# Two places of a fused FNet and MLP kernel rewritten: the first rows' way in, and the last column stage's order and stores

## The chip, the cores and the metric

The kernel runs on one core of a Trainium2 chip. The metric is the time of one execution on the device, in microseconds. TensorE (PE) multiplies, VectorE (DVE) and ScalarE (ACT) work on its results in PSUM and on SBUF, and SyncE (SP), ACT and GpSimd (POOL) issue the DMA transfers. Each engine runs its own list of instructions in order and waits on semaphores for the others.

## The reference

```python
def _A_ref(x, dft_seq_re, dft_seq_im, dft_hid_re, dft_hid_im):
    a = jnp.einsum("bsd,ed->bse", x, dft_hid_re)
    b = jnp.einsum("bsd,ed->bse", x, dft_hid_im)
    return jnp.einsum("ts,bse->bte", dft_seq_re, a) - jnp.einsum("ts,bse->bte", dft_seq_im, b)

def _B_ref(x, w1, b1, w2, b2):
    h = _gelu(jnp.einsum("bsd,df->bsf", x, w1) + b1)
    return jnp.einsum("bsf,fd->bsd", h, w2) + b2

xn = _layernorm(x, axis=-1)
return x + _A_ref(xn, ...) + _B_ref(xn, B_w1, B_b1, B_w2, B_b2)
```

x is 1 x 2048 x 640, the MLP's inner width 1536, and all is float32.

## The kernel before

**Head.** x comes in chunks of 128 rows, four to a tile. `load_x` (called in L698 and L699) loads chunks c0 to c3, the even ones on SP's queue, the odd ones on ACT's; behind them on SP go pieces of the first weight (`load_w1`, L258). PE runs twelve `warm_up` products of zeros (L715). The four chunks are centered (c0, c2 and c3 by `center` on DVE, L744; c1 on ACT), and 20 PE transposes of 128 x 128 (`transpose_x`, L732) put the centered rows into five PSUM banks `tacc[j]`, one for each 128 columns, with all four chunks side by side. `split` (L162 on ACT, L163 on DVE) then makes of each bank two fp32r numbers, a rounded half and the rest, and the first products (L302) read those. `split_first` (L765 on ACT, L766 on DVE) splits the first weight in the same way. Centers of c2 and c3 are made in two parts, columns 0 to 255 of both, and then, behind the weight's first split, the rest.

**Products.** A float32 product is made of three fp32r matmuls (L281, L282, L283: half by half, and the two cross terms), each with 512 columns of the moving operand and a 128 x 128 stationary one. The Fourier transform of the normed rows is made in stages: "s" stages transform along the sequence, "y" stages along the hidden width. Each stage is a 2 x 2 block product done with seven products (`NW` = 7) in place of eight, so that sums and differences of the blocks have to be formed beside it. `entries` lists (stage, product w, piece u); the loop at the end of the kernel goes through it: PE's matmuls (`sequence_entry` or `hidden_entry`), then the split of the piece three entries later (`form`, into one of the three buffers `as`), then the additions, transposes, loads and stores that `beside` or `hidden_beside` put at this entry. What stands in the code first is first in each engine's list.

A "y" stage has 21 entries: seven products of three pieces with 2, 2 and 1 of the five 128-row positions. The products sum into PSUM banks: X, Y and Z of two banks each, and US and VS of one. w = 0 and 1 also sum into US, w = 2 and 6 into VS. Matrices for a product at a position come through `load_g` in the order of the list `G`. In the last stage, w = 6 is done bank by bank: VS, then X, then X + 1, each with 15 matmuls of 512 columns.

**Tail.** `store` (L1372) writes a piece of a result block with four transfers, one for each quarter of the partitions, on the queues that it is given. Results of two row blocks (`ya` and `yo`, and the columns `ys` of the second) are added to what comes transposed out of PSUM by DVE (`turned`, `add_turned`). After the last matmul, the loop in L1825 to L1832 turns bank X + 1 whole and stores it. The framework gives each transfer of SP and ACT one of eight completion counters (DMAHW0 to DMAHW7), in the order of the code, and lets it wait for the transfer before it on that counter.

## Time and profile before

| | before |
|---|---|
| runs, median of 3 | 849.54 us (849.43 to 849.59) |
| the profiled execution | 849.81 us |
| its span | 848.0 us |
| instructions | 10383 |
| mean granted TensorE clock | 0.999 |

The page describes one execution. The span runs from its first instruction to its last, and 1.81 us of the profiled execution lie outside it. Busy time is given for each engine; PEld is PE's loading of the stationary operand, which overlaps the matmuls. The chain of work follows the last instruction back to what released it.

### The profile page before, as it was taken

The page shows a single profiled execution, that of the slowest core. Times are in us where ns is not written, and L with a number is a line of the kernel's source. Part 1 is how long each engine was busy: PE and PEld are TensorE (multiplying, and loading weights), DVE is VectorE, ACT ScalarE, POOL GpSimd, SP SyncE. Part 2 cuts the span into 40 slices and gives each one's busy share as a digit, 9 for nine tenths or more (in the row PEclk, how much of TensorE's full clock was granted, in tenths as well). Part 3 has the DMA queues.
Part 4 walks back from the last instruction along what each step waited for, and adds up shares of the span by engine and source line. Part 5 has one row for each costly group of instructions (what it writes and reads, how often), then busy time and mean ns, then how long its engine had stood idle before and what let it go on. Part 6 is the DMA issues. An engine that isn't in the chain of part 4 may idle for free.

```text
span 848.0 us, 10383 instructions
## 1 busy us (share of the span) xinstructions
PE 841.8 (99%) x3722; PEld 696.9 (82%) x3722; DVE 667.2 (79%) x855; ACT 355.7 (42%) x499; POOL 49.8 (6%) x70
## 2 busy tenths in 40 slices
PE   9999999999999999999999999999999999999997
PEld 8888888888888888888888888888888888888886
DVE  6765875686758878779988887889967988885687
ACT  7453644455665645433444343232323433223241
POOL 0000311031221400000000000000000000000001
PEclk9999999999999999999999999999999999999999
DMA  6758799537679989858644579563865779805364
GB/s 187 213 161 210 161 252 257 137 87 199 196 249 364 348 180 181 167 142 184 147 140 110 161 240 289 141 149 101 207 163 171 252 187 229 310 19 180 124 169 110
DMA packets 202435, 158.45 MB, mean 187 GB/s; under 512 B 75984, under 2 KB 175824, under 8 KB 201872
## 3 DMA queue, kind: packets, MB, share of 16 engines
q1 hardware_dynamic: 193696, 135.25, 62.1%
q0 software_dynamic: 4144, 21.24, 6.4%
q10 hardware_dynamic: 4544, 1.31, 0.6%
q8 instruction: 29, 0.48, 0.2%
q14 instruction: 22, 0.18, 0.1%
HBM read 114.76 MB, written 42.99 MB: 186 GB/s over the span
## 4 chain that ended last, share of the span: by engine, by line
PE 98%; DVE 1%; DMA 0%; issue 0%; DVEq 0%
PE banks L281 29%; PE banks L282 29%; PE banks L283 29%; PE banks L320 9%; PE banks L302 1%; DMA x<-in_A_x_dram 0%; DVE st L187 0%; DVE xp L744 0%; PE banks L352 0%; PE banks L355 0%; PE banks L353 0%; PE banks L732 0%; DVE yo L1829 0%; DVE mv L188 0%; PE banks L812 0%
## 5 line engine op out<-in xcount | busy, mean ns | idle before, releaser
L281 PE MATMUL banks<-as,xab 128*128 128x512 f32 x411 | 159.9, 389 | 0.0
L283 PE MATMUL banks<-as,xab 128*128 128x512 f32 x411 | 159.9, 389 | 0.0
L282 PE MATMUL banks<-as,xab 128*128 128x512 f32 x411 | 159.9, 389 | 0.0
L162 ACT ACTIVATE as<-r 128x1024 fp32r<-128x1024 f32 x80 | 85.0, 1062 | 177.7 <-PE banks L283 149.5
L163 DVE TENSOR_TENSOR as<-r,as 128x1024 fp32r<-128x1024 f32 x80 | 97.2, 1216 | 42.0 <-ACT as L162 42.0
L283 PEld LDWEIGHTS banks<-as,xab 128*128 128x128 f32 x411 | 77.2, 188 | 16.1
L281 PEld LDWEIGHTS banks<-as,xab 128*128 128x128 f32 x411 | 77.2, 188 | 16.0
L282 PEld LDWEIGHTS banks<-as,xab 128*128 128x128 f32 x411 | 77.2, 188 | 16.0
L281 PE MATMUL banks<-as,xc 128*128 128x512 f32 x224 | 87.1, 389 | 0.0
L282 PE MATMUL banks<-as,xc 128*128 128x512 f32 x224 | 87.1, 389 | 0.0
L283 PE MATMUL banks<-as,xc 128*128 128x512 f32 x224 | 87.1, 389 | 0.0
L162 ACT ACTIVATE as<-rt 128x1024 fp32r<-128x1024 f32 x32 | 34.0, 1063 | 70.5 <-PE banks L283 62.5
L320 PE MATMUL banks<-xtt,xab 128*128 128x512 f32 x210 | 50.0, 390 | 0.0
L283 PEld LDWEIGHTS banks<-as,xc 128*128 128x128 f32 x224 | 42.1, 188 | 8.8
L282 PEld LDWEIGHTS banks<-as,xc 128*128 128x128 f32 x224 | 42.1, 188 | 8.7
L281 PEld LDWEIGHTS banks<-as,xc 128*128 128x128 f32 x224 | 42.0, 188 | 8.7
L320 PEld LDWEIGHTS banks<-xtt,xab 128*128 128x128 f32 x210 | 39.4, 188 | 8.1
L163 DVE TENSOR_TENSOR as<-rt,as 128x1024 fp32r<-128x1024 f32 x32 | 38.8, 1212 | 5.3 <-ACT as L162 5.3
L162 ACT ACTIVATE as<-u 128x1024 fp32r<-128x1024 f32 (+1 forms) x24 | 22.1, 919 | 48.2 <-PE banks L283 48.2
L553 DVE STREAM_TRANSPOSE r<-raw 128x1024 f32<-128x1024 f32 x32 | 39.5, 1239 | 2.8 <-PE banks L283 2.2
L163 DVE TENSOR_TENSOR as<-u,as 128x1024 fp32r<-128x1024 f32 (+1 forms) x24 | 24.9, 1042 | 18.8 <-ACT as L162 18.8
L553 DVE STREAM_TRANSPOSE rt<-raw 128x1024 f32<-128x1024 f32 x32 | 38.8, 1230 | 0.9 <-PE banks L283 0.8
(364 smaller groups left out, 1635.7 us busy)
## 6 DMA issues: line engine op xcount, KB each, us to landing
raw<-in_A_dft_seq_re_dram SPq DMA_DIRECT2D x64, 256.0 KB, 5.4
raw<-in_A_dft_seq_im_dram SPq DMA_DIRECT2D x64, 256.0 KB, 5.0
ws<-wit SPq DMA_DIRECT2D x15, 384.0 KB, 5.0
xs<-x SPq DMA_DIRECT2D x64, 80.0 KB, 1.9
xo<-in_A_x_dram SPq DMA_DIRECT2D x16, 320.0 KB, 6.5
xab<-wit SPq DMA_DIRECT2D x13, 384.0 KB, 4.3
wit<-wstp POOLq DMA_DIRECT2D x12, 384.0 KB, 3.3
x<-in_A_x_dram SPq DMA_DIRECT2D x14, 320.0 KB, 4.6
```

The costliest lines, as they stand in the source:

```text
L162: nc.scalar.activation(h, s, AF.Copy)
L163: nc.vector.tensor_tensor(l, s, h.bitcast(F32), op=ALU.subtract)
L281: nc.tensor.matmul(acc, wh, mh, start=first, stop=False, skip_group_check=goes_on)
L282: nc.tensor.matmul(acc, wh, ml, start=False, stop=False, skip_group_check=goes_on)
L283: nc.tensor.matmul(acc, wl, mh, start=False, stop=last, skip_group_check=goes_on)
L302: nc.tensor.matmul(bank(g), W1[g][:, a, j * P : (j + 1) * P], XT[j][:, b], start=(j, k) == ends[0], stop=(j, k) == ends[-1],)
L320: nc.tensor.matmul(acc, W1[i][:, a, j * P : (j + 1) * P], XT[j][:, b], start=n == 0, stop=n == len(steps) - 1)
L553: nc.vector.transpose(held(pieces[g][2], u).rearrange("p c (n i) -> p c n i", i=B), r.rearrange("p n (c i) -> p c n i", i=B))
```

## The change

On the way in, all four chunks of x are loaded by SP; c2 is centered in one instruction, c3 in two, and the first weight's split comes after them; the transposes are taken chunk by chunk, with a warm-up behind c0 and c1. In the last column stage the products are taken in the order 1, 3, 4, 5, 6, 2, 7 (`order_of`). Two differences are formed in the stage before it (`moved_t2`) and kept beside the sums. What was added to a result after its transposition is now transposed early (`turn_ahead`, `turn_odd`) and put into the PSUM bank ahead of the products, by a copy on ACT or an add on DVE, so that the product goes on summing on it (`kept`, `goes_on`). The last product on X + 1 is split into two halves of 256 columns, and so are its transposition and its stores. Stores of `out_a`, of the odd columns and of the last pieces go to SP and ACT in turn; the second columns (`out_b` with k = 1) to SP alone.

```diff
+    def order_of(st):
+        return (0, 2, 3, 4, 5, 1, 6) if st == stages[-1] else tuple(range(NW))
+
+    entries = [(*st, w, u) for st in stages for w in order_of(st) for u in range(2 if st[0] == "s" else 3)]
...
+            src = A.get(("moved", w, u), src)
...
-        load_x(c, nc.scalar if c % 2 else nc.sync)
+        load_x(c)
...
-    def centers(j0, j1):
-        center(2, ALU.subtract, MV[:, 2, 0:1], j0, j1)
-        center(3, ALU.add, MV[:, 3, 5:6], j0, j1)
-
-    centers(0, 2)
+    center(2, ALU.subtract, MV[:, 2, 0:1])
+    center(3, ALU.add, MV[:, 3, 5:6], 0, 2)
+    center(3, ALU.add, MV[:, 3, 5:6], 2, ND)
     split_first(0, 2 * P)
-    centers(2, ND)
-    transpose_x(0, 0, ND)
-    transpose_x(1, 0, ND)
-    warm_up()
-    for j in range(2):
-        transpose_x(2, j, j + 1)
-        transpose_x(3, j, j + 1)
-    for c in (2, 3):
-        transpose_x(c, 2, ND)
+    for c in range(NC):
+        transpose_x(c, 0, ND)
+        if c < 2:
+            warm_up()
...
+            if p == 3:
+                post += {
+                    11: [lambda: turn_ahead(blocks[b - 1][1], 2, A["rt2"][:, 0, 0])],
+                    12: [lambda: turn_ahead(blocks[b - 1][1], 0, A["r01"][:, 0, 0]), lambda: turn_odd(t)],
+                    13: [lambda: moved_t2(b, 1)],
+                }.get(n, [])
...
+    def turn_ahead(t, c, dst):
+
+        nc.vector.transpose(
+            dst.rearrange("p c (n i) -> p c n i", i=B),
+            yo[t][:, :, c * B : (c + 2) * B].rearrange("p n (c i) -> p c n i", i=B),
+        )
+
+    def turn_odd(t):
+        nc.vector.transpose(A["r01"][:, 0, 1, 0].rearrange("p (n i) -> p n i", i=B), yo[t, 4])
+
+    def moved_t2(b, k):
+        t = blocks[b][1]
+        A["moved", 3, k] = A["r01"][:, 1, k]
+        add(A["r01"][:, 1, k], sums[t, KV[k]], sums[t, KU[k]], ALU.subtract)
...
+        def difference(k):
+            return A["moved", 3, k] if last and k < 2 else s(1, KU[k])
+
         def t3(k):
-            return lambda: add(s(0, KU[k]), s(1, KU[k]), s(0, KU[k]), ALU.subtract)
+            return lambda: add(s(0, KU[k]), difference(k), s(0, KU[k]), ALU.subtract)
 
         def t4(k):
-            return lambda: add(s(0, KV[k]), s(0, KV[k]), s(1, KU[k]), ALU.subtract)
+            def f():
+                dst = s(0, KV[k])
+                if last:
+                    dst = A["rt2"][:, (k + 1) // 2, (k + 1) % 2]
+                    dst = A["moved", 6, k] = dst if k < 2 else dst[:, 0]
+                add(dst, s(0, KV[k]), difference(k), ALU.subtract)
+
+            return f
...
+            if last:
+                return A["columns"][:, k]
...
+            return lambda: store(ta, ya[:, :, c0:c1], c0, c1, [nc.sync, nc.scalar] * 2) if last else None
...
+            if last:
+                yt = A["r01"][:, 0, 1, 1]
+                nc.vector.transpose(yt, us)
+                add_turned(ya[:, :, 4 * B :], yt)
+                out_a(4 * B, DQ)()
+                return
             yt = turned(us, f"yo_{tb}")
             add_turned(ya[:, :, 4 * B :], yt)
             add_turned(yo[tb, 4], yt)
-            out_a(4 * B, DQ)()
+
+        def last_odd():
+            nc.vector.transpose(yo[tb, 4], vs.rearrange("p (n i) -> p n i", i=B))
+            add_turned(yo[tb, 4], A["r01"][:, 0, 1, 1])
+            store(tb, yo[tb, 4], 4 * B, DQ, [nc.sync, nc.scalar] * 2)
+
+        def first_pair():
+            nc.vector.transpose(
+                ya[:, :, : 2 * B].rearrange("p n (e i) -> p e n i", i=B), y_.rearrange("p e (n i) -> p e n i", i=B)
+            )
+            out_a(0, 2 * B)()
+
+        def open_columns():
+            A["columns"] = place("xc01", (P, 2, NB, 2 * B), F32, name="columns")
+            load_yb(0)()
+            load_yb(1)()
...
-            return lambda: store(tb, columns(k), 2 * k * B, 2 * (k + 1) * B, [nc.gpsimd] * Q if last else None)
-
-        def last_two():
-
-            acc, yt = s(1, "v1"), A["yt"](f"yb2_{tb}")
-            d = columns(1).rearrange("p n (e i) -> p e n i", i=B)
-            v1()
-            for n in range(2):
-                m = slice(n * TB // 2, (n + 1) * TB // 2)
-                for e in range(2):
-                    nc.vector.transpose(yt[:, e, m], acc[:, e, m])
-                dn = d[:, :, n * NB // 2 : (n + 1) * NB // 2]
-                add(dn, dn, yt[:, :, m].rearrange("p e (n i) -> p e n i", i=B))
-                queues = [nc.sync, nc.scalar] * 2
-                store(tb, columns(1), 2 * B, 4 * B, queues, n * NB // 2, (n + 1) * NB // 2)
-                if n == 0:
-                    end()
-
-        def last_columns():
-
-            A["end"] = A["rt2"][:, 0, 0, 0]
-            nc.vector.transpose(A["end"].rearrange("p (n i) -> p n i", i=B), ya[:, :, 3 * B : 4 * B])
+            return lambda: store(tb, columns(k), 2 * k * B, 2 * (k + 1) * B, [nc.gpsimd] * Q if last and k == 0 else None)
...
-        pre = [v1] if n == 17 and not last else []
+        if last:
+            held0, held4 = A["r01"][:, 0, 0], A["r01"][:, 0, 1, 0]
+            post = {
+                0: [
+                    lambda: gather(1, tb, "v1", z_),
+                    lambda: gather(1, tb, "v", vs, op=ALU.subtract),
+                    lambda: moved_t2(b, 0),
+                ],
+                1: [open_columns, copy(vs, held4), t3(1)],
+                2: [t2(2), t3(0)],
+                3: [lambda: add(held0, held0, x_)],
+                4: [copy(y_, held0), t3(2), t4(1)],
+                5: [t4(0)],
+                6: [copy(s(1, "v1"), z_), t4(2)],
+                9: [copy(s(1, "v2"), x_)],
+                12: [lambda: add(s(1, "v2"), s(1, "v2"), z_)],
+                13: [yb1],
+                14: [yb1],
+                15: [v1, yb2],
+                16: [lambda: add(x_, x_, A["rt2"][:, 0, 0]), yb2],
+                18: [first_pair, odd],
+                19: [last_odd],
+            }.get(n, [])
...
+        g0 = order_of(("y", (blocks[b - 1][1], blocks[b][1]))).index(w) * ND
+
+        def use_g(acc, j, pos, first, stop, goes_on=False, m=slice(0, TB)):
             r, k = (n - u + (pos // 2)) % 3, pos % 2
             a = A["as"][:, r]
-            use(acc, GT[b, w * ND + pos], j, a, k, first, stop, goes_on)
+            use(acc[:, m], GT[b, g0 + pos], j, a[:, :, :, m], k, first, stop, goes_on)
 
         def wide(j, pos):
-            use_g(bank(where + j), j, pos, w < 3 and pos == 0, pos == ND - 1, w > 2)
+            kept = w > 2 or (last and w == 1)
+            use_g(bank(where + j), j, pos, not kept and pos == 0, pos == ND - 1, kept)
...
-                    use_g(bank(VS), 2, pos, False, pos == ND - 1)
+                    use_g(bank(VS), 2, pos, False, pos == ND - 1, True)
                 for pos in range(ND):
                     wide(0, pos)
             elif u == 1:
-                for pos in range(ND):
-                    wide(1, pos)
+                for m in (slice(0, TB // 2), slice(TB // 2, TB)):
+                    for pos in range(ND):
+                        use_g(bank(X + 1), 1, pos, False, pos == ND - 1, True, m)
             return
...
-                use_g(bank(VS), 2, pos, pos == 0, False)
+                use_g(bank(VS), 2, pos, pos == 0 and not last, False, last)
...
     t = blocks[-2][1]
-    for k, queues in ((2, [nc.sync, nc.scalar] * 2), (3, [nc.sync, nc.scalar] * 2)):
+    for k, n0, n1 in ((2, 0, NB), (3, 0, NB // 2), (3, NB // 2, NB)):
         d = yo[t][:, :, k * B : (k + 1) * B]
-        if k == 3:
-            nc.vector.transpose(d, bank(X + 1).rearrange("p (n i) -> p n i", i=B))
-        else:
-            add_turned(d, turned(bank(X), f"yt_{k}"))
-        store(t, d, k * B, (k + 1) * B, queues=queues)
+        nc.vector.transpose(d[:, n0:n1], bank(X + k - 2)[:, n0 * B : n1 * B].rearrange("p (n i) -> p n i", i=B))
+        store(t, d, k * B, (k + 1) * B, [nc.sync, nc.scalar] * 2, n0, n1)
```

How it moves instructions, at three places. In the lists a row is line, operation, result and operand, shape, and how many stand in a row.

PE at the start of the program, up to the first products, as a difference (before -, after +); `zeros` are the warm-ups, `xp` the centered rows, `xtt` the split transposed ones:

```order
-L1859 UNCONDITIONAL_BRANCH
-L715 MATMUL banks<-zeros 128x128 x12
-L732 MATMUL banks<-ident,xp 128x128 x10
-L715 MATMUL banks<-zeros 128x128
-L732 MATMUL banks<-ident,xp 128x128 x10
+L1912 UNCONDITIONAL_BRANCH
+L720 MATMUL banks<-zeros 128x128 x12
+L737 MATMUL banks<-ident,xp 128x128 x5
+L720 MATMUL banks<-zeros 128x128
+L737 MATMUL banks<-ident,xp 128x128 x5
+L720 MATMUL banks<-zeros 128x128
+L737 MATMUL banks<-ident,xp 128x128 x10
```

A warm-up more stands between the transposes, and the blocks of c2 are all ahead of those of c3.

DVE's last instructions, before; `as` is the split's buffer, `v_1_2_5580` the sum whose columns are stored second, in brackets what an instruction waits for:

```order
L163 TENSOR_TENSOR as<-v_1_1_5297,as 128x1024 [waits Activation_49]
L493 TENSOR_TENSOR u_1_2_5314<-u_1_2_5314,yb_2_5961 128x2x16x32 [waits DMAHW0_49,DVE_49]
L163 TENSOR_TENSOR as<-v_1_1_5122,as 128x1024 [waits Activation_49]
L163 TENSOR_TENSOR as<-v_1_5280,as 128x512 [waits Activation_49]
L493 TENSOR_TENSOR v_1_2_5580<-v_1_2_5580,banks 128x1024 [waits PE_49]
```

And after, with the end of the list (L1884 is the loop behind the last product):

```order
L163 TENSOR_TENSOR as<-rt_2826,as 128x1024 [waits Activation_49]
L493 TENSOR_TENSOR banks<-banks,rt_2826 128x1024
L493 TENSOR_TENSOR columns<-columns,yb_2_5962 128x2x16x32 [waits DMAHW5_49,DVE_49]
L163 TENSOR_TENSOR as<-rt_2826,as 128x512 [waits Activation_49]
L1696 STREAM_TRANSPOSE yo_5255<-banks 128x2x16x32
L1682 STREAM_TRANSPOSE r_2747<-banks 128x512 [waits PE_49]
L493 TENSOR_TENSOR yo_5255<-yo_5255,r_2747 128x16x32 [waits DVE_49]
L1691 STREAM_TRANSPOSE y_2_5547<-banks 128x512 [waits PE_49]
L493 TENSOR_TENSOR y_2_5547<-y_2_5547,r_2747 128x512 [waits DVE_49]
L1884 STREAM_TRANSPOSE yo_5255<-banks 128x16x32 [waits PE_49]
L1884 STREAM_TRANSPOSE yo_5255<-banks 128x8x32 [waits PE_49]
L1884 STREAM_TRANSPOSE yo_5255<-banks 128x8x32
```

Two adds of 1024 elements a partition came between the splits of the second and third piece of the last product; of the two transposes of the last bank only the first waits for PE.

SP's last stores, before:

```order
L1372 DMA out_dram<-y_2_5547 32x16x32 [waits DMAHW3_49,DVE_49]
L1372 DMA out_dram<-y_2_5547 32x16x32 [waits DMAHW5_49]
L1372 DMA out_dram<-yo_5255 32x16x32 [waits DMAHW7_49,DVE_49]
L1372 DMA out_dram<-yo_5255 32x16x32 [waits DMAHW1_49]
L1372 DMA out_dram<-yo_5255 32x16x32 [waits DMAHW3_49,DVE_49]
L1372 DMA out_dram<-yo_5255 32x16x32 [waits DMAHW5_49]
```

SP's last six, after:

```order
L1370 DMA out_dram<-yo_5255 32x16x32 [waits DMAHW0_49,DVE_49]
L1370 DMA out_dram<-yo_5255 32x16x32 [waits DMAHW1_49]
L1370 DMA out_dram<-yo_5255 32x8x32 [waits DMAHW2_49,DVE_49]
L1370 DMA out_dram<-yo_5255 32x8x32 [waits DMAHW3_49]
L1370 DMA out_dram<-yo_5255 32x8x32 [waits DMAHW4_49,DVE_49]
L1370 DMA out_dram<-yo_5255 32x8x32 [waits DMAHW5_49]
```

And ACT's last six, after:

```order
L1370 DMA out_dram<-yo_5255 32x16x32 [waits DMAHW6_49,DMAHW5_49,DVE_49]
L1370 DMA out_dram<-yo_5255 32x16x32 [waits DMAHW7_49]
L1370 DMA out_dram<-yo_5255 32x8x32 [waits DMAHW0_49,DVE_49]
L1370 DMA out_dram<-yo_5255 32x8x32 [waits DMAHW1_49]
L1370 DMA out_dram<-yo_5255 32x8x32 [waits DMAHW3_49,DVE_49]
L1370 DMA out_dram<-yo_5255 32x8x32 [waits DMAHW4_49]
```

Before, SP's stores have the odd counters and ACT's the even ones. After, SP has three more of the last stores, two smaller ones stand where one stood, and both queues use the counters 0, 1, 3 and 4.

More of the change, by code (lines that the diff above doesn't have):

```diff
@@ L1567, in beside @@
         return pre, post
+    def turn_ahead(t, c, dst):
[9 more added lines that the diff above has]
+        add(A["r01"][:, 1, k], sums[t, KV[k]], sums[t, KU[k]], ALU.subtract)
     CHUNKS = ((0, 2), (1, 3), (4,))
-    G = [(w, c) for w in range(NW) for cs in CHUNKS for c in cs]
+    G = {
+        b: [(w, c) for w in order_of(("y", (blocks[b - 1][1], blocks[b][1]))) for cs in CHUNKS for c in cs]
+        for b in (NT + 1, NT + 3)
+    }
     GT = {}
@@ L1642, in out_a @@
         def out_a(c0, c1):
-            return lambda: store(ta, ya[:, :, c0:c1], c0, c1) if last else None
+            return lambda: store(ta, ya[:, :, c0:c1], c0, c1, [nc.sync, nc.scalar] * 2) if last else None
         def odd():
+            if last:
[4 more added lines that the diff above has]
+                return
             yt = turned(us, f"yo_{tb}")
@@ L1683, in last_columns @@
-        def last_columns():
-            A["end"] = A["rt2"][:, 0, 0, 0]
-            nc.vector.transpose(A["end"].rearrange("p (n i) -> p n i", i=B), ya[:, :, 3 * B : 4 * B])
-        yb1, yb2 = in_two(0), in_two(1)
-        yb4 = to(
-            yo[tb, 4], vs, f"yb4_{tb}", lambda: store(tb, yo[tb, 4], 4 * B, DQ, queues=[nc.sync, nc.scalar] * 2 if last else None)
-        )
-        f5s = [lambda u=u: f5(u) for u in range(2)] if not last else [lambda: None] * 2
-        f6s = [lambda u=u: f6(u) for u in range(2)] if not last else [lambda: None] * 2
@@ L1694, in hidden_beside @@
-        v1 = lambda: add(s(1, "v1"), s(1, "v1"), x_)
-        end = lambda: add(bank(X + 1), bank(X + 1), A["end"])
-        pre = [v1] if n == 17 and not last else []
+            return lambda: store(tb, columns(k), 2 * k * B, 2 * (k + 1) * B, [nc.gpsimd] * Q if last and k == 0 else None)
+        yb1, yb2 = in_two(0), in_two(1)
+        yb4 = to(yo[tb, 4], vs, f"yb4_{tb}", lambda: store(tb, yo[tb, 4], 4 * B, DQ))
+        f5s = [lambda u=u: f5(u) for u in range(2)]
+        f6s = [lambda u=u: f6(u) for u in range(2)]
@@ L1697, in hidden_beside @@
+        pre = [v1] if n == 17 else []
         post = {
```

45 lines of the change are left out of this document (21 added, 24 removed).

## The prediction

> **What bounds the kernel now.** I read the page first, then the chain of work that ended last, at both ends.
>
> ```profile
> span 848.0 us, 10383 instructions
> PE 841.8 (99%) x3722; PEld 696.9 (82%) x3722; DVE 667.2 (79%) x855; ACT 355.7 (42%) x499; POOL 49.8 (6%) x70
> ...
> PE 98%; DVE 1%; DMA 0%; issue 0%; DVEq 0%
> ...
> L281 PE MATMUL banks<-as,xab 128*128 128x512 f32 x411 | 159.9, 389 | 0.0
> ```
>
> TensorE is busy 99% of the span, the chain is 98% PE, and the costliest group has no idle time before it (last column 0.0). So the end moves only with what happens before the first matmul, with a new gap or dearer matmuls in PE's list, and with what follows the last matmul. Those are two short stretches of the chain:
>
> ```profile
> 0.73 3.77 DMA x<-in_A_x_dram
> ...
> 5.69 0.55 DVE xp L744
> ...
> 8.66 0.88 PE banks L732 x6
> 9.53 2.54 PE banks L302 x11
> ```
>
> ```profile
> 842.90 0.24 PE banks L283
> 843.14 0.02 issue
> 843.17 0.72 DVE yo L1829
> ```
>
> The first columns are start and length in us. x chunk 0 lands at 0.73 + 3.77 = 4.50, and the products begin near 9.3. Call the end of the last matmul E = 843.14. Behind it stand one transpose of 512 columns (done at E + 0.75) and its four stores. A pitch of 0.2267 us for a 512-column matmul comes from the same chain (842.90 to 843.14, rows of 0.23 and 0.24).
>
> The stores, by the line's own view and the queues' timeline:
>
> ```profile
> L1372 SPq DMA_DIRECT2D out_dram<-yo x4: 315/397/506, 842.5 to 844.3; - x4
> L1372 ACTq DMA_DIRECT2D out_dram<-yo x4: 374/442/538, 842.5 to 844.3; - x4
> ...
> DMA to landing us min/median/max: 1.9/2.4/2.6
> ```
>
> An issue takes about 0.42 us of its queue, a store lands 1.9 to 2.6 us after its start, the last starts at 844.3. So the last lands at about 844.3 + 2.6 = 846.9, E + 3.8, and the span ends 1.1 later. Profiled, the execution took 849.81, against the runs' median of 849.54. I form differences against the profiled one and put them on the median.
>
> **Head.** In the trace, c0 and c1 are transposed together, and c2 and c3 wait for DVE's centering:
>
> ```profile
> 6.39 1.31 PE L732 MATMUL banks<-ident,xp 128*128 128x128 f32 x10
> ```
>
> ```profile
> 7.54 0.39 PE L715 MATMUL banks<-zeros 128*128 128x128 f32 x2
> 7.77 1.77 PE L732 MATMUL banks<-ident,xp 128*128 128x128 f32 x10
> 9.29 0.70 PE L302 MATMUL banks<-xtt,xab 128*128 128x512 f32 x2
> ```
>
> ```profile
> 7.32 0.62 DVE L744 TENSOR_SCALAR xp<-x,mv 128x256 f32<-128x256 f32 x2
> 7.85 0.42 DVE L766 TENSOR_TENSOR xab<-w1r,xab 128x256 fp32r<-128x256 f32 x1
> 8.18 0.75 DVE L744 TENSOR_SCALAR xp<-x,mv 128x384 f32<-128x384 f32 x2
> ```
>
> DVE ends its four centerings at 8.93. The change takes the weight's split (0.42) from between them and makes c2's two pieces one instruction of 640 (0.55, L744 in the chain above): 7.32 + 0.55 + 0.31 + 0.38, less some overlap, is 8.45, so DVE is 0.48 earlier. But PE's order now limits. Ten transposes took 6.39 to about 7.48, a pitch of 0.11; a warm-up (two passes, 7.54 to 7.77) costs 0.23 and a gap of 0.06. The new order is c0, warm-up, c1, warm-up, c2, c3. From 6.39, where the long warm-up still lets c0 begin: c0 to 6.94, c1 7.23 to 7.77, c2 8.0 to 8.54, c3 8.54 to 9.09. Before, the first block of c3 went in just before ACT's first copy; that copy needs blocks (2,0) and (3,0):
>
> ```profile
> 8.36 1.09 ACT L162 ACTIVATE xtt<-banks 128x512 fp32r<-128x512 f32 x2 [0.71 <-PE banks L732]
> 9.33 0.53 ACT L765 ACTIVATE xab<-w1r 128x384 fp32r<-128x384 f32 x1
> 9.74 1.57 ACT L162 ACTIVATE xtt<-banks 128x512 fp32r<-128x512 f32 x3
> ```
>
> Block (3,0) now ends at 8.54 + 0.28 (one transpose in flight) = 8.82, so the copy starts at 8.85 instead of 8.36, and everything on ACT behind it (five copies, one weight split, back to back) moves by 0.49. The first matmul follows the copy's first half (0.55): about 9.45 instead of 9.29. Then the copies, not PE, set the first products, and the matmuls of the third and fifth copies come about 0.4 late. **Head: +0.4.** Lower bound: were the copies no limit, matmuls would follow the transposes at 9.09, −0.2. Upper bound: the whole 0.49 and one more gap, +0.6.
>
> The loads: x1 and x3 leave ACT's queue for SP's. DMA was full at that time (the last two columns below are its share and GB/s), so one queue instead of two carries the same bytes; and were x earlier, PE, held by the warm-ups until 6.39, would not begin sooner. I put this at nothing; it lies within the bounds above.
>
> ```profile
> 3.00:3.50 0.50, 0.50 (x4) 0.50 (x4) 0.00 (x0) 0.16 (x1) 0.00 (x0) 1.00 1.03 415
> ...
> 4.00:4.50 0.50, 0.50 (x4) 0.50 (x4) 0.00 (x0) 0.00 (x0) 0.00 (x0) 1.00 1.04 415
> ```
>
> **Last column stage, DVE.** Its last splits (w = 6 of the seven products) in the trace:
>
> ```profile
> 829.47 1.25 DVE L1395 STREAM_TRANSPOSE yb<-v 128x1024 f32<-128x1024 f32 x1
> 830.64 1.18 DVE L163 TENSOR_TENSOR as<-v,as 128x1024 fp32r<-128x1024 f32 x1
> 831.74 1.21 DVE L493 TENSOR_TENSOR u<-u,yb 128x1024 f32<-128x1024 f32 x1
> 832.87 1.82 DVE L163 TENSOR_TENSOR as<-v,as 128x1024 fp32r<-128x1024 f32 x2
> ...
> 835.86 0.77 DVE L1675 STREAM_TRANSPOSE yb<-v 128x256 f32<-128x256 f32 x2
> ```
>
> ```profile
> 831.58 1.06 ACT L162 ACTIVATE as<-v 128x1024 fp32r<-128x1024 f32 x1 [1.66 <-PE banks L283]
> ```
>
> The row with x2 is the split of the second piece and, right behind it, of the third (512). ACT's half of the second piece begins when PE gives the buffer free, R = 831.58, and DVE's half can start at R + 1.10. The order after puts two adds of 1024 (into PSUM, and into the columns) between these two splits. With starts 1.14 apart (829.47, 830.64, 831.74, 832.87), the third split starts at R + 1.10 + 3 × 1.14 = R + 4.52, ends 0.69 later, and PE can use it at R + 5.25. PE wants it at its 23rd matmul after R: nine of product 2's last piece, twelve of the first four positions, and one. A matmul gives its buffer free at its end, 0.39 after its start, so that is R + 22 × 0.2267 − 0.16 = R + 4.83. **Stall: +0.42, I take +0.45.** Bounds 0.2 (1.06 apart) and 0.6 (an add into PSUM dearer by 0.15). What waits behind it is PE itself, so all of it goes to the end. The other splits of the stage keep their cover: between them DVE has no more than one add and one transpose, as here, and product 2 sums into three banks, so that PE has 18 matmuls there for a piece of two positions rather than 12. The adds and transposes that left the end (turning of US and VS, the sums from G) run beside PE and buy nothing.
>
> **Smaller matmuls.** The last product's 15 matmuls of 512 become 30 of 256; nothing else in PE's list changes its number. The trace has no 256. Half of 0.2267 is 0.113, no cost. Shortest rows are the transposes, 128 columns at a pitch of 0.11, each with a weight load of its own:
>
> ```profile
> 6.36 1.10 PEld L732 LDWEIGHTS banks<-ident,xp 128*128 128x128 f32 x10
> ```
>
> So loads keep up at 0.11, and a straight line between the two pitches gives 0.148, +1.05. The dearest is 0.2267, +3.4. I take 0.12, near half since the loads keep up: 30 × 0.12 − 3.40 = **+0.2**, with 0 and 1.05 as bounds; the dearest is a rival.
>
> The Trainium skill, "TensorE: Matmul & The Clock Gate", section "Back-to-back issue gap", gives an isolated gap of N/2.4 + 2.5 ns, an estimate of 109 ns at 256 and −0.1 us for the 30; it also gives 131 ns as sustained at 512, where the trace has 0.2267, so I follow the row.
>
> **Tail.** The bank of the last product is to be transposed and stored in two halves of 256. But of the two transposes in the order, the first waits for PE and the second has no wait; so the first waits for the last matmul, and nothing begins before E. Two transposes of 256 take 0.77 together (row at 835.86): the first is done at E + 0.43, the second at E + 0.8.
>
> The Trainium skill, "PSUM — Partial Sum Buffer", section "PSUM bank collisions raise a hardware error", has one engine read a bank only while no other writes it, whatever the columns; the row shown agrees (the transpose starts 0.03 behind the last matmul).
>
> What then decides are the eight completion counters (DMAHW0 to 7 in the order) that SP and ACT share: each transfer waits until the one before it on its counter has landed. The head shows this:
>
> ```profile
> 4.52 0.31 SPq L258 DMA_DIRECT2D w1r<-in_B_w_dram  x1
> ```
>
> ```profile
> SPq L258 <- DMA x<-in_A_x_dram: 1.5, 2, 0.7
> ```
>
> The first weight load on the counter of x0 is issued at 4.52, right behind x0's landing at 4.50, and such loads waited 1.5 us for x. Before, the last stores alternate between SP and ACT on the counters and find them free. After, the four column stores are all SP's, and the counts that the waits hold put ACT's last four stores ahead of SP's on four counters: SP's last six (two of k = 2, two each of the halves of k = 3) wait on 0, 1, 2, 3, 4, 5, where 0 and 1 are those of ACT's stores of the first half, 3 and 4 of its second half. SP can't begin even k = 2, which is ready before E, until ACT's store has landed. With issues of 0.42 and a landing of 2.15 (half the old size, between the least and the median): ACT issues at E + 0.48, landed E + 2.63; SP issues at E + 2.67 and five more at 0.42, the last at E + 4.77, landed E + 6.92. The later counters (E + 3.95 for the fourth) come in time. Against E + 3.8: **+3.1**. Bounds: 1.9 and 0.40 give E + 6.3, +2.5; 2.6 and 0.50 give E + 8.2, +4.4.
>
> **Sum.** 0.4 + 0.45 + 0.2 + 3.1 = +4.15: 849.81 becomes 853.96 for a profiled execution, 849.54 becomes **853.7** for the median. The lower bounds together give +2.5 (852.0), the upper +6.65 (856.2).
>
> **Rivals.** (A) Not slower: SP's stores find their counters free, because SP comes to them only after ACT's stores have landed or the shared counters don't bind stores of two queues. Then SP and ACT issue two stores each for k = 3 from E + 0.48, the last at E + 1.9, landed E + 4.15: tail +0.35, sum +1.4, 850.9. It decides where ACT's first-half store lands before SP is through with its earlier stores; for that it would have to land about 2 us sooner. For it: behind 843 SP's stores wait for DVE alone, not for a transfer (below). Against it: there the counters alternate, and the load in the head did wait for x0. Chance 0.10.
>
> ```profile
> SPq L1372 <- DVE yo L1829: 0.5, 1, 0.5
> ```
>
> (B) A 256-column matmul costs what a 512 costs: +3.2 more, 856.9. For it: no row of 256; against it: the pitch of 0.11 at 128. Chance 0.06. (C) The first half is read while the second is summed: its data are there 15 × 0.12 = 1.8 before E, ACT's first store lands at E + 0.8 and SP's first three go then; its other three wait for ACT's store of the second half (landed E + 2.63), the last at E + 3.5, landed E + 5.65: tail +1.85, sum +2.9, 852.4. Against it stands the missing second wait. Chance 0.03.
>
> **How the numbers follow.** Forecast 0.78, A 0.10, B 0.06, C 0.03, and 0.03 for something not seen, mostly faster. A measurement of this kernel tells about 0.2%, 1.7 us, from no change (847.8 to 851.2). A lies within, the forecast, B and C above. The range takes in the forecast with its bounds and A: 850.8 to 856.2, the forecast's own is 852.0 to 856.2. Faster 0.02, same 0.11, slower 0.87. The most that could be gained, head −0.2 and the first half stored early, is far below 1.7.
>
> **What would show it.** First L302 matmul near 9.45 and ACT's first copy at 8.85; one gap of 0.4 to 0.5 in PE some 7.5 us before its end; 30 matmuls 0.12 apart; SP idle for some 2 us behind E on a DMA of out, then six issues in a row. If SP issues its k = 2 stores before E, the tail is wrong and A is the case; if the 30 take 6.8, B is.

## The result and the profile after

| | before | after |
|---|---|---|
| median of the runs | 849.44 us (849.25 to 849.59) | 853.91 us (853.75 to 854.73) |
| the profiled execution | 849.81 us | 853.75 us |
| its span | 848.0 us | 852.0 us |

The ratio is 1.0054, with a 95% interval of 1.0044 to 1.0065: the change costs 4.5 us. From here on E is the end of the last matmul, and the tail is the time from E to the landing of the last store, both from the trace's records of matmuls and transfers. The page of the kernel after, with the lines that answer to those of before (busy times, and the shares of the chain that ended last):

```profile
span 852.0 us, 10412 instructions
...
PE 842.8 (99%) x3739; PEld 698.3 (82%) x3739; DVE 666.2 (78%) x849; ACT 357.1 (42%) x501; POOL 49.9 (6%) x70
...
PE 97%; DMA 1%; DVE 0%; ACT 0%; issue 0%; SPq 0%; DVEq 0%
```

PE's busy time grew by 1.0 us, the span by 4.0: most of the loss is not work. The chain of the kernel after, at its start (start, length):

```profile
2.12 5.37 DMA x<-in_A_x_dram
7.48 0.02 issue
7.51 0.58 ACT ab L743
...
8.37 0.36 DVE xp L749
...
9.15 0.60 ACT xtt L162
9.75 0.04 issue
9.80 2.37 PE banks L302 x8
```

It no longer begins with x0 but with x3, which landed at 7.48 (6.45 before). The first product starts at 9.80 instead of 9.29. In DVE's and ACT's timelines the same place reads:

```profile
8.37 0.68 DVE L749 TENSOR_SCALAR xp<-x,mv 128x256 f32<-128x256 f32 x2 [0.50 <-ACT ab L743]
```

```profile
7.51 0.74 ACT L743 ACTIVATE ab<-x 128x640 f32<-128x640 f32 x1 [1.06 <-DMA x<-in_A_x_dram]
...
9.15 1.09 ACT L162 ACTIVATE xtt<-banks 128x512 fp32r<-128x512 f32 x2 [0.40 <-PE banks L737]
```

ACT waits for x3 and sums it, and DVE stands 0.50 us until that sum is there before it can center c3. Near the end, the chain has the gap and the halves:

```profile
836.57 0.50 PE banks L282
837.06 0.23 PE banks L283
...
840.72 0.12 PE banks L281
...
844.19 0.13 PE banks L283
844.32 0.03 issue
844.34 0.45 DVE yo L1884
```

PE's waits in the same kernel name the releaser, and DVE's timeline shows what it did before:

```profile
PE banks L282 <- DVE as L163: 0.3, 1, 0.3
```

```profile
832.42 1.23 DVE L163 TENSOR_TENSOR as<-rt,as 128x1024 fp32r<-128x1024 f32 x1 [0.45 <-ACT as L162]
833.56 1.23 DVE L493 TENSOR_TENSOR banks<-banks,rt 128x1024 f32<-128x1024 f32 x1
834.70 1.22 DVE L493 TENSOR_TENSOR columns<-columns,yb 128x1024 f32<-128x1024 f32 x1
835.83 0.68 DVE L163 TENSOR_TENSOR as<-rt,as 128x512 fp32r<-128x512 f32 x1
```

The split of the third piece comes behind both adds; against the pace ahead of it, PE is 0.56 us late behind the gap (0.45 in the wait, 0.11 in the next matmul). The thirty halves start between 840.55 and 844.02, 0.12 apart. At the end, SP's queue from 840 on and its waits from 838 on:

```profile
840.60 3.92 SPq L1370 DMA_DIRECT2D out_dram<-yo  x4
844.62 0.98 SPq L1370 DMA_DIRECT2D out_dram<-y  x2
846.73 3.03 SPq L1370 DMA_DIRECT2D out_dram<-yo  x6
```

```profile
SPq L1370 <- DMA out_dram<-yo: 5.3, 4, 2.6
SPq L1370 <- DMA out_dram<-y: 1.0, 1, 1.0
```

SP's last six stores begin 2.4 us behind E. The landings tell what SP waited for: the first of the six starts at 846.73, 0.06 behind the landing (846.67) of the store that ACT had issued at 844.82 on the same counter, and the second at 847.42, 0.02 behind the landing of ACT's next one; the other four follow in a row. SP was late before E already: its longest wait, 2.6 us up to 840.60, was for a store of ACT's too, landed at 840.54. Every run, by its profiled execution (one each, so that small differences between rows can be chance):

| kernel | first product | E | last landing | tail | time |
|---|---|---|---|---|---|
| before | 9.29 | 843.13 | 846.96 | 3.83 | 849.81 |
| before, once more (b0_again) | 9.27 | 842.76 | 846.55 | 3.80 | 849.41 |
| after | 9.80 | 844.30 | 850.96 | 6.66 | 853.75 |
| a1_two_queues | 9.59 | 844.35 | 851.00 | 6.65 | 853.82 |
| b1_one_queue | 10.21 | 844.23 | 848.07 | 3.84 | 850.93 |
| a2_alternate | 9.61 | 846.27 | 850.31 | 4.04 | 853.19 |
| a3_pool | 10.11 | 844.62 | 850.54 | 5.92 | 853.68 |
| a4_whole | 9.43 | 843.79 | 848.99 | 5.20 | 852.04 |
| a5_split_first | 9.62 | 844.08 | 850.83 | 6.75 | 853.63 |
| a6_both | 10.16 | 844.28 | 850.20 | 5.92 | 853.06 |
| d1_less_bytes | 9.62 | 843.50 | 847.25 | 3.75 | 850.11 |
| d3_pair_cut | 9.78 | 844.27 | 851.57 | 7.30 | 854.40 |
| c1_best | 9.27 | 843.00 | 849.09 | 6.09 | 851.98 |
| c3_before_plus | 8.96 | 842.95 | 846.93 | 3.98 | 850.08 |

### The profile page after: what moved, and what is told of

It reads as the page before. It is cut to its first block, busy times and chain, and to the rows that moved or that the text cites. A ratio compares the mean times of both kernels' runs of the same rounds, so it can differ in the third digit from the quotient of the medians.

```text
span 852.0 us, 10412 instructions
## 1 busy us (share of the span) xinstructions
PE 842.8 (99%) x3739; PEld 698.3 (82%) x3739; DVE 666.2 (78%) x849; ACT 357.1 (42%) x501; POOL 49.9 (6%) x70
## 4 chain that ended last, share of the span: by engine, by line
PE 97%; DMA 1%; DVE 0%; ACT 0%; issue 0%; SPq 0%; DVEq 0%
PE banks L282 29%; PE banks L283 29%; PE banks L281 29%; PE banks L320 9%; PE banks L302 1%; DMA x<-in_A_x_dram 1%; SPq L180 0%; DVE banks L493 0%; PE banks L353 0%; PE banks L355 0%; PE banks L352 0%; DVE columns L493 0%; ACT as L162 0%; ACT ab L743 0%; DVE as L163 0%
## 5 line engine op out<-in xcount | busy, mean ns | idle before, releaser
L162 ACT ACTIVATE as<-r 128x1024 fp32r<-128x1024 f32 x82 | 87.1, 1062 | 185.0 <-PE banks L283 153.8
L282 PE MATMUL banks<-as,xab 128*128 128x512 f32 (+1 forms) x415 | 160.6, 387 | 0.3 <-DVE as L163 0.3
L281 PE MATMUL banks<-as,xab 128*128 128x512 f32 (+1 forms) x415 | 160.5, 387 | 0.0
L283 PE MATMUL banks<-as,xab 128*128 128x512 f32 (+1 forms) x415 | 160.5, 387 | 0.0
L163 DVE TENSOR_TENSOR as<-r,as 128x1024 fp32r<-128x1024 f32 x82 | 99.6, 1216 | 44.4 <-ACT as L162 44.3
L282 PEld LDWEIGHTS banks<-as,xab 128*128 128x128 f32 x415 | 78.0, 188 | 16.5 <-DVE as L163 0.7
L281 PEld LDWEIGHTS banks<-as,xab 128*128 128x128 f32 x415 | 78.0, 188 | 15.8
L283 PEld LDWEIGHTS banks<-as,xab 128*128 128x128 f32 x415 | 78.0, 188 | 15.7
L162 ACT ACTIVATE as<-rt 128x1024 fp32r<-128x1024 f32 (+1 forms) x35 | 36.8, 1050 | 78.0 <-PE banks L283 70.0
L163 DVE TENSOR_TENSOR as<-rt,as 128x1024 fp32r<-128x1024 f32 (+1 forms) x35 | 41.9, 1197 | 7.1 <-ACT as L162 7.1
L493 DVE TENSOR_TENSOR r<-r,rt 128x1024 f32<-128x1024 f32 x32 | 38.9, 1218 | 0.1
L344 DVE TENSOR_TENSOR hs<-ab,hs 128x512 fp32r<-128x512 f32 x24 | 17.4, 725 | 25.8 <-ACT hs L342 25.8
```

Source lines behind the costliest of these rows:

```text
L162: nc.scalar.activation(h, s, AF.Copy)
L163: nc.vector.tensor_tensor(l, s, h.bitcast(F32), op=ALU.subtract)
L281: nc.tensor.matmul(acc, wh, mh, start=first, stop=False, skip_group_check=goes_on)
L282: nc.tensor.matmul(acc, wh, ml, start=False, stop=False, skip_group_check=goes_on)
L283: nc.tensor.matmul(acc, wl, mh, start=False, stop=last, skip_group_check=goes_on)
L344: nc.vector.tensor_tensor(hs[:, 1], a, hs[:, 0].bitcast(F32), op=ALU.subtract)
```

## The experiments

**The kernel before, once more.** No edit.

> The kernel before, unchanged, profiled once more. In its first profile PE stood still for 0.4 us at 671.7 us behind a weight load that landed at 672.00; in the changed kernel's profile that wait is missing, and so its head cost 0.82 us up to there and 0.42 us behind it. Theory 'chance of the transfers': the wait is of another length here, or missing, and other short waits may be there; the first product still starts at 9.3 and the tail still ends 3.8 us behind the last matmul. Rival 'always there': a wait of 0.4 us at 671.7 again, and then a kernel that starts later gets these 0.4 us back each time.

The wait was missing, as the first theory had it, and E came 0.37 us earlier than in the first profile. In the first profile the chain had it so:

```profile
671.79 0.23 PE banks L283
672.02 0.12 issue
672.14 0.47 PE banks L281
```

In the second, no matmul between 668 and 673 is late:

```profile
671.80 0.23 PE banks L283
672.02 0.23 PE banks L281
672.25 0.23 PE banks L282
```

Like waits, which cost 0.2 to 0.5 us, end between 670 and 673.3 in a1_two_queues, b1_one_queue, a2_alternate and a5_split_first, and in none of the others; in a5_split_first PE's waits name the releaser:

```profile
PE banks L281 <- DMA ws<-wit: 0.3, 1, 0.3
```

So it comes and goes with the run; in the one profile that names its cause it is a load that lands late. Matmuls are counted here from the first that reads the split rows (L302). Against b0_again the change loses 0.83 us up to the 300th matmul (it starts at 77.60 against 76.77), 0.56 in the gap, 0.19 in the halves, in sum 1.58 (E differs by 1.55), and 2.86 in the tail.

**Two queues for x in the changed kernel.**

```diff
-        load_x(c)
+        load_x(c, nc.scalar if c % 2 else nc.sync)
```

> The changed kernel with x1 and x3 loaded by ACT again; all else as changed. Theory 'one queue': the single queue lets x3 land at 7.48 instead of 6.45, and that alone makes the first product start at 9.80. Then x3 lands near 6.45 here, the first product starts at about 9.45 (what the order of the transposes costs, by the prediction), and the matmuls of the first stage stand 0.4 us behind those of the kernel before instead of 0.82. Rival 'order': the loads don't matter, the first product starts at 9.8 here too.

x3 landed at 6.53, and the first product started at 9.59 (9.45 was expected); the 300th matmul stood 0.60 us behind b0_again's. ACT's first copy, by its timeline:

```profile
8.94 1.09 ACT L162 ACTIVATE xtt<-banks 128x512 fp32r<-128x512 f32 x2 [1.24 <-PE banks L737]
```

Now it waited 1.24 us for PE's transposes alone. That is the limit which the prediction named, at 8.94 instead of 8.85, since the transposes began at 6.49 (x0 landed at 4.60). But 0.60 lies within what the eight kernels with one queue and the new order show, +0.44 (a4_whole) to +1.17 (a6_both). Neither theory holds as stated: both limits are there, and close together. The eight tell them apart: where x3 landed by 7.31 (four profiles) the head cost 0.44 to 0.67, about as much as here; where it landed at 7.46 to 7.48 (two) 0.79 and 0.83, and at 7.80 (two) 1.15 and 1.17.

**One queue for x in the kernel before.** The same edit the other way round.

> The kernel before with all four chunks of x loaded by SP; centers and transposes in the order before. Theory 'one queue': x3 lands near 7.5, ACT's sum of it ends near 8.35, and the first product starts about 0.7 us later than before, 9.9 to 10.1. Rival 'order': x3 may land later, but the first product starts within 0.1 us of 9.29.

x3 landed at 7.50, the first product started at 10.21 (9.9 to 10.1 was expected), and the 300th matmul was 0.92 late. The queue alone does it; in the old order, which centers c3 in two parts with the weight's split between, it cost in this one profile as much as the whole new head. In all nine profiles with one queue x0 landed at 3.6 to 3.9 and x3 at 7.0 to 7.8, in the five with two queues x0 at 4.5 to 4.6 and the last of c2 and c3 at 6.2 to 6.5. Why the last chunk comes so late, with the same bytes ahead of it, stays open: the windows of the kernel after show 307 and 271 GB/s from 3.5 to 4.5, where before had 405 and 415.

**Second columns stored by SP and ACT in turn.**

```diff
-            return lambda: store(tb, columns(k), 2 * k * B, 2 * (k + 1) * B, [nc.gpsimd] * Q if last and k == 0 else None)
+            return lambda: store(tb, columns(k), 2 * k * B, 2 * (k + 1) * B, [nc.gpsimd] * Q if last and k == 0 else [nc.sync, nc.scalar] * 2 if last else None)
```

> The changed kernel with the four stores of the second columns given to SP and ACT in turn instead of SP alone. SP's stores then have the odd counters and ACT's the even ones up to the end. Theory 'shared counters': SP's last six stores no longer wait for ACT's; the last store lands 4.0 to 4.3 us behind the last matmul instead of 6.6, the span is 2.3 to 2.6 us shorter (849.5) and the time about 851.4. Rival 'long queue': SP is late because it has 16 stores to issue; with two fewer it gains two issues, 0.9 us, and the time is about 853.0.

The tail fell to 4.04 as foreseen, but E went to 846.27: PE has a gap of 1.8 us, and more behind it. The median, 853.25, is 1.0046 of before's (1.0030 to 1.0063), where 851.4 us was expected. PE's waits name ACT, and ACT's timeline shows why:

```profile
PE banks L281 <- ACT as L162: 1.6, 1, 1.6
```

```profile
836.08 0.95 ACTq L1370 DMA_DIRECT2D out_dram<-columns  x2
837.12 0.63 ACT L162 ACTIVATE as<-rt 128x512 fp32r<-128x512 f32 x1 [4.61 <-issue]
```

ACT's two column stores stand in its list ahead of its half of the third split, and they wait for DVE's add. Work that PE needs sat behind a store. The short tail proves nothing yet: PE's gap gave the earlier stores time to land.

**Second columns on POOL; both mends at once.** In the first, `[nc.gpsimd] * Q if last`. The second has the alternating stores, and:

```diff
-                16: [lambda: add(x_, x_, A["rt2"][:, 0, 0]), yb2],
+                16: [lambda: add(x_, x_, A["rt2"][:, 0, 0])],
+                17: [yb2],
```

> The changed kernel with the four stores of the second columns on POOL's queue, as the first columns'. SP and ACT then alternate on the eight counters, and nothing new stands in ACT's list. Theory 'shared counters': no new gap of PE, and the last store lands 4.0 to 4.2 us behind the last matmul instead of 6.66; the time is about 851.4. Rival 'the stores themselves are slow' (in the run with alternating queues every store landed 2 to 3.5 us after its issue): the tail stays above 5.5 us and the time above 852.7.

> The changed kernel with both: second columns stored by SP and ACT in turn, and their last add put behind the split of the third piece, so that ACT's stores stand behind its half of that split. Theory: the gap of 1.8 us that the alternating stores alone brought came from ACT, whose two column stores waited for DVE's add ahead of the half of the third piece; so here there is no gap at all, the tail is 4.0 to 4.2, and the time is 850.7 to 851.0 (0.8 of it the head, 0.2 the smaller matmuls). Rival: the gap is the price of more stores at once; then 0.5 us or more of it stays and the time is above 851.5.

Neither tail fell to 4.2: 5.92 in both, as the rival of a3_pool had it. a6_both had no gap near the end, as its theory said, and its ratio to before was 1.0041 (1.0027 to 1.0055). With the counters in turn, ACT's and SP's stores of a6_both took longer to land (the line's own view, from 835 on; 1.6/2.2/3.1 in the kernel after), and the windows of 2 us show the transfers full (last two columns: share of the DMA engines, here above 1, and GB/s):

```profile
DMA to landing us min/median/max: 1.8/3.2/4.6
```

```profile
842.00:844.00 2.00, 2.00 (x19) 2.00 (x18) 0.00 (x0) 0.00 (x0) 0.00 (x0) 1.00 1.41 202
844.00:846.00 2.00, 0.28 (x3) 0.07 (x1) 0.78 (x2) 0.00 (x0) 0.00 (x0) 1.00 1.51 174
846.00:848.00 2.00, 0.00 (x0) 0.00 (x0) 0.00 (x0) 0.00 (x0) 0.00 (x0) 0.99 1.27 149
```

The theory of the shared counters alone falls. Nor are the counters free in a6_both: each queue now waits for a store of its own.

```profile
SPq L1370 <- DMA out_dram<-yo: 2.4, 5, 0.7
```

SP's store at 843.94, for example, went 0.06 us behind the landing (843.87) of SP's own store before it on that counter. With eight counters eight stores are on their way, and the next one goes when the oldest has landed; what holds the end is how fast they land.

**The last product whole.** `for m in (slice(0, TB),)`, and the last loop with (3, 0, NB) in place of the two halves.

> The changed kernel with the last product, its transposition and its stores whole: 15 matmuls of 512 columns instead of 30 of 256, one transposition, four stores. By the prediction the last product takes 3.40 us instead of 3.60, so the last matmul ends 0.2 earlier. SP then has six stores behind counters as before, but only two of them (k = 3) on counters that ACT's stores of k = 3 use: the tail is 5.0 to 5.6 us instead of 6.66, and the time about 852.5. Rival 'halving helps the tail': the whole transposition and the larger stores cost more than the shorter chain saves, and the time is 853.7 or more.

From the 3400th matmul to E it took 0.19 us less, the price of the halves; the tail was 5.20, the time 852.04, as the theory said. The halving of the stores costs more than the halving of the matmuls. (k = 2 and k = 3 are the last two column blocks, those of banks X and X + 1.) Here SP's stores of k = 2 go at 844.38 and 844.85, ahead of any wait for ACT's stores of k = 3, and only its last two wait for those (the first landed at 846.63, SP's next began at 846.70). In the kernel after, six stores stand behind that wait.

**The split ahead of the columns' add.** The edit of a6_both's second part alone.

> The changed kernel with the last add into the second columns put behind the split of the third piece on DVE. Theory: the gap of 0.45 us in PE at 835.9 (with 0.11 more behind it) goes, the last matmul ends 0.5 us earlier as counted from the matmul ahead of the gap, the tail behind it stays at 6.5 to 6.8, the time is about 853.4. Rival: the gap comes from ACT's half of the split or from a load; then it stays, at 0.4 to 0.5.

The gap went, and from the 3400th matmul to E it took 0.59 us less. DVE's timeline:

```profile
833.93 1.23 DVE L493 TENSOR_TENSOR banks<-banks,rt 128x1024 f32<-128x1024 f32 x1
835.06 0.68 DVE L163 TENSOR_TENSOR as<-rt,as 128x512 fp32r<-128x512 f32 x1
```

The tail stayed at 6.75. The time, 853.63, holds the 0.5 us of the wait for a load that ends at 670.21 (above).

**Fewer bytes.** Same number of stores; those of the second columns and the first pair write 2 of 16 row blocks (the first pair alone in the second run). The rest of these columns is left out of the output. d1_less_bytes has the alternating queues and the split first, d3_pair_cut the changed kernel's queues and order. The line that both change for the first pair:

```diff
-            out_a(0, 2 * B)()
+            store(ta, ya[:, :, : 2 * B], 0, 2 * B, [nc.sync, nc.scalar] * 2, 0, 2)
```

> The kernel with alternating stores and the split put first, with the same number of stores on the same queues and counters, but those of the second columns and of the first pair write 2 of their 16 row blocks only; the rest of these columns of the output is left out. Theory 'backlog': the stores that the new order pushed into the last 8 us keep the transfers busy (one lands every 0.4 us from 839.5 to 850.2, whatever the counters), so that with some 0.9 MB less to write the later stores land 1.7 to 2.6 us after their issue instead of 3 to 4.5, and the last one 3.8 to 4.4 us behind the last matmul instead of 5.92; the time is 851.0 to 851.7. Rival 'number of stores': 28 issues and eight counters set the end; then the tail stays above 5.4 us.

> The changed kernel, stores on the queues as changed, but the four stores of the first pair write 2 of their 16 row blocks; the rest of these columns of the output is left out. SP's last six stores have the counters 0 to 5 again, and its second one of k = 2 shares counter 1 with ACT's store of the first half. Theory 'two limits': with 0.45 MB less to write the transfers are no longer the limit, but the shared counters alone still hold SP: its second store of k = 2 goes when ACT's store of the first half has landed (2.4 to 2.7 us behind the last matmul), four more follow at 0.42, and the last lands 5.6 to 6.1 us behind the last matmul. Rival 'backlog alone': the shared counters only showed the backlog; with fewer bytes the tail falls to 4.5 us or less.

d1_less_bytes: tail 3.75, a little below the theory's, and landings at a median of 1.8 us where a6_both had 3.2:

```profile
DMA to landing us min/median/max: 1.4/1.8/3.2
```

So what held a6_both was what the stores carry, not their number. Bytes and rows were cut together here, so the runs don't tell which of the two counts. d3_pair_cut: landings as short (1.5/1.8/2.3), no backlog, and yet a tail of 7.30, where the theory had 5.6 to 6.1; SP's waits from 840 on:

```profile
SPq L1370 <- DMA out_dram<-yo: 4.5, 3, 2.2
```

Its last six stores started 3.1 us behind E. The theory had SP's second store of k = 2 wait for ACT's store of the first half. That wait stood three stores earlier in SP's list, at its first store of the odd columns (tile `y`): it starts at 846.39, 0.06 behind the landing (846.33) of ACT's store, and seven more stand behind it. So the counters weren't taken as in the kernel after, although the list of stores is the same. Nor were they taken there in the order of the code, as the description of the kernel before has it: ACT's stores of k = 3 hold counters 0, 1, 3 and 4 ahead of SP's stores of k = 2, which stand before them in the code. How long a tail the counters of the kernel after would leave with fewer bytes is therefore not shown.

Still, each of the two limits alone keeps the tail near 6 us or above; only without both does it come back to that of before.

**Everything mended at once.** Head as before, alternating stores, the split first, and the last product's second half in bank Z:

```diff
+                add(xs_[:, m], xs_[:, m], es[:, m])
+                add(bank(Z)[:, : TB // 2], xs_[:, 3 * TB // 2 :], es[:, 3 * TB // 2 :])
...
+                        use_g(bank(Z if m.start else X + 1), 1, pos, False, pos == ND - 1, True, m, slice(0, TB // 2))
```

> The changed kernel with everything mended that was found before: head as in the kernel before, alternating stores, the split ahead of the columns' add, and the second half of the last product summed in a bank of its own, so that the first half is turned and stored 1.8 us earlier. Theory 'backlog': no gap in PE, the head costs nothing, but the last store is held by the stores ahead of it: the last landing moves by the head's 0.8 us alone, to 849.2 to 849.6, and the time is 852.0 to 852.5. Rival 'the wait for the whole bank': the early half frees the end, the tail falls to 2.8 to 3.3 us, and the time is 849.3 to 849.8.

First product at 9.27, no gap; DVE turned the first half ahead of the last matmul:

```profile
841.24 0.45 DVE L1900 STREAM_TRANSPOSE yo<-banks 128x256 f32<-128x256 f32 x1 [0.79 <-PE banks L283]
843.04 0.45 DVE L1900 STREAM_TRANSPOSE yo<-banks 128x256 f32<-128x256 f32 x1 [1.34 <-PE banks L283]
```

But its stores queued behind the others: turned by 841.69, the first half was first stored at 844.49. Tail 6.09, median 851.97, ratio 1.0030 (1.0018 to 1.0042). The backlog decides, as the theory said.

**The kernel before with three small edits** (the weight's split behind all centers, the fifth block's sum put into PSUM at n = 9, the last product in two banks).

> The kernel before, its product order and early stores kept, with three small edits: the weight's first split behind all centers; the fifth column block's sum put into PSUM ahead, so that one add goes from the end of DVE's list; and the last product in two halves in two banks. Theory: the first product starts 0.2 to 0.3 us earlier (9.0), the halves cost 0.2 us on PE, the last store lands 3.0 to 3.6 us behind the last matmul instead of 3.8; in sum 0.1 to 0.7 us faster than before, 848.8 to 849.4. Rival: sixteen issues in place of twelve on two queues take back what the smaller last stores give, and ACT's copies hold the head; then the time is 849.4 to 849.9.

The rival's reasons held, and the time was longer than even its range: 850.16, ratio 1.0007 (0.9998 to 1.0016), no difference that shows. The first product started at 8.96, but the 30th matmul only 0.05 us earlier than in b0_again (15.96 against 16.01), as ACT's copies did (8.31 and 9.70 against 8.34 and 9.73). Sixteen last stores in place of twelve came with a tail of 3.98. No version was found that beats the kernel before.

## Why the prediction was right, and where it was not

Forecast 853.7, measured 853.91, inside the range of 850.8 to 856.2; +4.15 forecast, +4.47 measured. By its steps, against b0_again:

- **Head, +0.4 forecast, +0.83 measured, beyond its upper bound of 0.6.** (The eight profiles with this head have 0.44 to 1.17, on average 0.79, and seven of them lie above 0.6.) The step that failed is "The loads: ... I put this at nothing": in one queue x3 lands 1.0 us later, and DVE and ACT wait for it, which b1_one_queue shows alone (+0.92); the bounds, which were to take it in, were worked out from PE and the copies only. The step on PE's order and ACT's first copy stands: with two queues it alone gives +0.60, against the 0.4 forecast; the transposes began 0.10 later than taken. The two overlap, since they delay the same copy.
- **Gap on DVE, +0.45 forecast, +0.56 measured.** The cause is as named: with the split first it goes, all else alike. The 0.11 is the slower matmul behind the wait, which the sum left out.
- **Halves, +0.2 forecast, +0.19 measured**, at 0.12 apiece.
- **No overlap with the half bank.** The first transposition started 0.04 us behind E (844.34), as the missing second wait said. Rival C's early half came in c1_best, with banks of its own, and gained nothing in a tail that is full.
- **Tail, +3.1 forecast, +2.86 measured.** SP's last six stores started at E + 2.4 and E + 5.0 for the last (forecast 2.67 and 4.77), and the last landed at E + 6.66 (6.92). The last landings took 1.65 us instead of 2.15, and the six went out 0.52 apart instead of 0.42, since the second waited 0.4 us for another store of ACT's. The mechanism is real: SP's starts follow ACT's landings, and d3_pair_cut has it with fewer bytes. But rival A, "SP's stores find their counters free" with "tail +0.35", left out a second condition (and by its own terms the last store lands at E + 4.05, not 4.15). With no counter shared (a3_pool, a6_both) the tail is still 5.92; only with fewer bytes as well do ACT and SP issue as A has it, the last at E + 1.95, and the tail is 3.75 (d1_less_bytes). The prediction counted the stores' issues and counters and never the bytes that the new order moves into the last 8 us.

Where these bytes came from shows in the views of the store's line. Before, from 790 to 836:

```profile
L1372 SPq DMA_DIRECT2D out_dram<-yo x8: 337/486/636, 811.2 to 815.9; - x8
```

These eight stores (the first pair and the fifth block) went out some 30 us ahead of E. In the new order the product that completes them is the last but one, and the same eight go out between 837.7 and 844.2: SP and ACT have 28 stores of 2.1 MB in all from 835 on, against 20 of 1.3 MB before. The rows they write are of 128 or 256 bytes; while they fill the DMA engines, 150 to 200 GB/s move (windows above), where the head's loads in rows of 2560 bytes moved 415. The Trainium skill, "DMA: Bandwidth & Descriptors", section "Specifications", puts the least transfer for full rate at 512 B; the two rates agree with it. But the one is of stores and the other of loads, so that no run here shows the length of the rows alone to be the cause.

That the forecast came out so near is in part luck: the misses of the head (0.43 too little) and the gap (0.11) and that of the tail (0.24 too much) went opposite ways. And nothing in the tail's time told of the limit that was left out: the two are of like height (6.66 with both, 5.92 with the bytes alone), and the one that was counted hid the other.

## What to carry to other kernels

A wait that is taken out shows the next one: before a price is put on "this limit gone", look for a second limit of the same height, here the bytes of the stores behind the counters of their queues. Count for each reordering what it moves towards the end, in transfers and in bytes, and not only what it adds. And where a queue's transfers share their completion counters with another queue's, or a store stands in a compute engine's list ahead of work that others need, the lists of the queues with their waits, and not the order of the code alone, tell which store stands behind which.

## What the runs showed of the hardware that was not expected

- Four loads of 320 KB in one queue land one after the other, at 3.78, 4.73, 6.13 and 7.48, where in two queues they land at 4.50, 4.67, 6.04 and 6.45: the first earlier, the last a full microsecond later.
- With eight of them in flight, stores of 64 KB in rows of 128 bytes landed one every 0.4 us (a6_both, from 843.9 to 848.3; a3_pool and c1_best alike), each 3.1 to 4.2 us behind its issue; with few in flight a store of 32 KB landed 1.6 us behind it (the last ones of the kernel after).
- Matmuls of 256 columns, with a weight load each, follow one another at 0.12 us (the thirty halves of the kernel after), and the first matmul behind a wait of PE is 0.08 to 0.11 us longer than the rest: 0.34 us to the next start at 836.57 in the kernel after, 0.31 at 672.14 in the kernel before, where the others take 0.227.
